# Batch 1's queries loaded four tokens a partition in a retention and GELU-MLP kernel on one Trainium2 core

## The chip, the core and the metric

The kernel runs on one core of a Trainium2 chip. The metric is the device time of one execution in microseconds (us). Before the change the median of 11 runs is 298.6 us, the lowest 297.46 and the highest 299.8. Engines are called as in the profile: PE (matmuls), PEld (its weight loads), DVE (vector), ACT (scalar), POOL (GpSimd), SP (the queue that issues the DMAs).

## What is computed

Eight batches of eight heads, 576 tokens, head dimension 64. First a retention attention: scores with a decay mask, times the values. Its result, tokens by 512, goes through an MLP with 2048 hidden columns and a tanh GELU.

```python
scores = scale * np.matmul(q, k.transpose(0, 1, 3, 2))
gamma = 1.0 - 2.0 ** (-5.0 - np.arange(H, dtype=np.float32))
Dmat = np.where(rel >= 0, gamma[:, None, None] ** rel[None, :, :], 0.0)
ret = scores * Dmat[None, :, :, :]
attn = np.matmul(ret, v)
x = attn.transpose(0, 2, 1, 3).reshape(B * S, H * D)
h = x @ w_in
g = 0.5 * h * (1.0 + np.tanh(c * (h + 0.044715 * h * h * h)))
out = g @ w_out
```

Inputs and output are float32; on the chip the operands of the matmuls are float16.

## The kernel before, in words

**Tiling.** The first 512 tokens of a batch are split in two halves `s` of 256, each in two chunks `c` of 128; the last 64 tokens of each batch are a "tail" that is handled apart. The eight heads are two groups `hh` of four, and a group is two head pairs `pp`. Per half and group, `load_qkv` (L192) fetches 256 KB of q, k or v into a float32 tile; `cast_qk` (L249) or `cast_v` (L258) makes float16 of it and gives the float32 tile back; `tr` (L356) transposes four 128-column blocks on PE and copies them out of PSUM to the tile `T`; `score_mm` (L428) makes the scores of one half and group; `mask_sc` (L446, DVE) multiplies the mask in; `values` (L543) multiplies with v. The part of the past goes through a running state: `state_mm` (L490), `scan` (L513, DVE), `put` (L533, a cast of the state to the block-diagonal tile `tbd`), `inter_mm` (L573). `evac` (L592, DVE) moves the result of a chunk out of PSUM to the tile `x`. Then a block of the MLP: `up` (L633) or `up_half` (L720) with the GELU on ACT, sums and differences of the hidden columns (`mix_sa`, `mix_sc`, `mix_d`, L740 to L754), and seven products with combinations of w_out (`product`, L763, `down`, L866), whose results `settle` (L794) adds up.

**Two layouts of a load.** Normally a partition receives two consecutive tokens of each of four heads (`r=2`), a run of 512 bytes per head. For the pairs in the set `R4` (L128) it receives four consecutive tokens of each of two heads (`r=4`), a run of 1024 bytes; the index `s` of such a load and of its cast and transpose then stands for the head pair, not for the half of the tokens. One such tile feeds both halves, so both tiles of a group, `s` 0 and 1, are needed before the first scores of that group. Its transposes are copied out in two copies of 128x256 instead of one of 128x512. When k is loaded so, `back` (L414) transposes it back for `state_mm`; q needs nothing of the kind.

**What sets the order.** Nothing is scheduled at run time. A list `units` (L1024 to L1027) gives the main work of PE: units 0 to 9 are empty (L1024), 10 and 11 are `up_half` of block 0, 14 to 25 its `up(4)` to `up(15)`, 26 to 41 block 1's `up_half`, 42 to 48 and 49 to 55 the `down` products of blocks 0 and 1, 56 to 71 `up` of block 2, 72 to 78 its products. A dictionary `plan` (L1028 to L1372) hangs further steps behind each unit, each with its engine: A is ACT, V is DVE, G is POOL, S2 is half on ACT and half on DVE. Within a unit the list's order counts. Each engine executes its own queue strictly in this order. Later blocks have a plan of the same kind in a loop (L1378 to L1533).

**Loads.** All loads go through SP's one queue in the order of the calls L903 to L985. A load needs either one of 12 tiles `ld` (L163), which a cast gives back, or a home borrowed from a tile not yet in use (`E`, `E2`, `O`, `H`, L897 to L901 and L1022).

**Padding.** `pads` (L988 to L1014) puts dummy matmuls of 128 columns (`pad`, L145, their line is L150) in front of named steps of batch 0, and `warm(16)` puts some at the start.

Of the kernel before, what the change touches and what calls it, by code (L numbers as in the profile page):

```python
# [19 lines left out]
def kernel(  # L20
# [24 lines left out]
    B, H, S, D = q.shape  # L45
# [52 lines left out]
    sc = const.tile([128, 2 * H + 4], F32, name="sc")  # L98
# [29 lines left out]
    R4 = {(0, "k"), (0, "q")}  # L128
# [762 lines left out]
    def add(plan, *entries):  # L891
# [9 lines left out]
    H = []  # L901
# [15 lines left out]
    load_w_in(0, 2, E)  # L917
# [3 lines left out]
    load_w_in(2, 1, None)  # L921
    load_w_in(1, 0, E2)
# [4 lines left out]
    load_qkv(1, 0, 0, "q", None)  # L927
    load_w_in(2, 3, None)
# [3 lines left out]
    load_qkv(1, 0, 1, "q", None)  # L932
    load_w_in(3, 3, None)
    load_w_in(3, 1, None)
    load_w_in(3, 2, None)
    load_qkv(1, 0, 1, "v", None)
    load_qkv(1, 1, 0, "k", O)
    load_qkv(1, 1, 0, "q", O)
    load_qkv(1, 1, 1, "k", O)
    load_w_out(0, None)  # L940
    load_qkv(1, 1, 0, "v", O)
    load_qkv(1, 1, 1, "q", O)
    load_qkv(1, 1, 1, "v", O)
    load_w_out(1, None)
    load_w_out(6, E3)
    load_w_out(2, None)
# [3 lines left out]
    load_w_out(14, H)  # L950
    load_w_out(7, E3)
    load_w_out(8, O)
    load_w_out(10, H)
    load_w_out(11, H)
    load_w_out(12, H)
    load_w_out(9, O)
    load_w_out(15, H)
# [3 lines left out]
    load_qkv(2, 0, 0, "q", None)  # L961
    load_qkv(2, 0, 0, "k", None)
    load_qkv(2, 1, 0, "q", None)
    load_qkv(2, 0, 1, "q", None)
    load_qkv(2, 0, 0, "v", None)
# [23 lines left out]
        ("tr", 0, 1, 0, 0): 7,  # L989
        ("tr", 0, 1, 1, 0): 0,  # L990
        ("tr", 0, 1, 1, 1): 1,
        ("st", 0, 1, 0): 1,
# [4 lines left out]
        ("bk", 0, 1, 1): 0,  # L997
        ("us", 0, 0): 4,
        ("us", 0, 1): 4,
        ("xs", 0, 0): 7,  # L1000
        ("xs", 0, 1): 0,
        ("in", 0, 3): 0,
        ("tr", 0, 0, 0, 0): 9,
        ("tr", 0, 0, 0, 1): 10,
        ("tr", 0, 0, 1, 0): 23,
        ("tr", 0, 0, 1, 1): 5,
# [3 lines left out]
        ("tr", 0, 1, 0, 1): 5,  # L1010
        ("in", 0, 1): 11,
        ("us1", 0, 1): 0,
        ("in", 0, 2): 7,
# [6 lines left out]
    def turn():  # L1020
# [7 lines left out]
    plan = add({},  # L1028
        (0, L(cast_qk, 0, 0, 0, "q", A)),
        (0, L(new_x, 0)),  # L1030
# [9 lines left out]
        (3, L(score_mm, 0, 1, 0)),  # L1040
        (2, L(back, 0, 0, 0, V)),
# [4 lines left out]
        (2, L(back, 0, 1, 0, A)),  # L1046
        (1, L(tr, 0, 0, 1, 0, S2)),
        (1, L(cast_qk, 0, 1, 1, "q", G)),
        (5, L(back, 0, 0, 1, A)),
        (3, L(tr, 0, 0, 1, 1, A)),  # L1050
        (1, L(cast_qk, 0, 1, 1, "k", G)),
# [4 lines left out]
        (4, L(score_mm, 0, 0, 1)),  # L1056
        (4, L(cast_v, 0, 0, 0, G)),
        (5, L(scan, 0, 0)),
        (5, L(values, 0, 0)),
        (6, L(score_mm, 0, 1, 1)),  # L1060
        (6, L(put, 0, 0, A)),
        (3, L(cast_v, 0, 0, 1, G)),
        (5, L(scan, 0, 1)),
        (1, L(inter_mm, 0, 0, 0)),
        (5, L(put, 0, 1, A)),
# [6 lines left out]
        (6, L(cast_v, 0, 1, 1, G)),  # L1072
        (7, L(state_mm, 0, [1])),
        (5, L(cast_v, 0, 1, 0, G)),
        (7, L(scan, 0, 2)),
# [7 lines left out]
        (11, L(scan, 0, 3)),  # L1083
        (9, L(evac, 0, 1, 1)),
        (7, L(cast_w_in, 0, 3, A)),
        (9, L(F0.up_half, 0, 0)),
        (8, L(cast_w_in, 0, 1, G)),
        (8, L(cast_w_in, 0, 0, G)),
        (11, L(put, 0, 3, V)),
        (9, L(F0.up_half, 1, 0)),  # L1090
        (12, L(cast_qk, 1, 0, 0, "k", G)),
        (14, L(cast_w_in, 2, 3, G)),
        (12, L(cast_qk, 1, 0, 1, "k", V)),
        (7, L(cast_w_in, 1, 3, A)),
        (10, L(cast_w_in, 2, 1, A)),
        (8, L(cast_w_in, 1, 1, A)),
        (13, L(F0.mix_sc, 0, 2, V)),
# [3 lines left out]
        (9, L(cast_w_in, 2, 0, V)),  # L1101
        (18, L(F0.mix_d, 0, 2, V)),
        (7, L(turn)),
        (7, L(cast_w_in, 1, 2, A)),
        (19, L(F0.mix_sc, 2, 2, V)),
        (10, L(cast_qk, 1, 0, 0, "q", A)),
        (18, L(cast_qk, 1, 0, 1, "q", V)),
        (19, L(cast_w_in, 3, 0, A)),
        (19, L(tr, 1, 0, 1, 1, A)),
        (15, L(tr, 1, 0, 1, 0, S2)),  # L1110
        (15, L(tr, 1, 0, 0, 0, S2)),
        (17, L(cast_w_in, 3, 2, G)),
# [4 lines left out]
        (28, L(inter_mm, 1, 0, 0)),  # L1117
# [7 lines left out]
        (22, L(state_mm, 1, [0])),  # L1125
        (21, L(score_mm, 1, 0, 1)),
        (24, L(cast_qk, 1, 1, 0, "k", G)),
# [4 lines left out]
        (21, L(cast_qk, 1, 1, 0, "q", A)),  # L1132
        (22, L(values, 1, 0)),
        (29, L(put, 1, 1, A)),
        (23, L(cast_qk, 1, 1, 1, "q", A)),
        (25, L(cast_v, 1, 1, 0, V)),
        (27, L(F0.mix_sc, 4, 2, G)),
        (25, L(tr, 1, 1, 0, 0, V)),
# [3 lines left out]
        (22, L(F0.mix_sa, 4, 2, G)),  # L1142
        (27, L(cast_v, 1, 1, 1, V)),
        (24, L(tr, 1, 1, 0, 1, A)),
        (28, L(state_mm, 1, [1])),
        (28, L(F0.mix_d, 4, 2, V)),
        (27, L(tr, 1, 1, 1, 0, A)),
# [3 lines left out]
        (27, L(tr, 1, 1, 1, 1, A)),  # L1151
# [4 lines left out]
        (29, L(mix_w_out, 0, "sums", G)),  # L1156
# [3 lines left out]
        (31, L(inter_mm, 1, 1, 0)),  # L1160
        (32, L(mix_w_out, 1, "sums", G)),
        (28, L(mix_w_out, 1, "copy", A)),
        (34, L(mix_w_out, 1, "add", G)),
        (33, L(mix_w_out, 2, "sums", G)),
        (32, L(evac, 1, 1, 0)),
        (32, L(mix_w_out, 3, "sub", V)),
        (37, L(mix_w_out, 3, "copy", A)),
        (33, L(evac, 1, 1, 1)),
        (33, L(mix_w_out, 2, "add", V)),
        (37, L(mix_w_out, 3, "sums", V)),  # L1170
        (33, L(mix_w_out, 1, "sub", V)),
        (40, L(mix_w_out, 7, "add", V)),
        (37, L(mix_w_out, 0, "copy", A)),
        (36, L(mix_w_out, 0, "add", V)),
        (40, L(mix_w_out, 4, "sums", V)),
        (34, L(mix_w_out, 2, "copy", A)),
        (34, L(mix_w_out, 2, "sub", V)),
        (37, L(mix_w_out, 6, "sums", V)),
        (35, L(mix_w_out, 4, "sub", V)),
        (38, L(mix_w_out, 5, "sub", V)),  # L1180
        (43, L(mix_w_out, 4, "add", V)),
        (38, L(mix_w_out, 5, "add", V)),
        (38, L(mix_w_out, 4, "copy", V)),
# [3 lines left out]
        (40, L(mix_w_out, 6, "add", V)),  # L1187
        (36, L(mix_w_out, 7, "sub", V)),
        (33, L(mix_w_out, 6, "copy", A)),
        (42, L(cast_qk, 2, 0, 0, "q", A)),  # L1190
        (29, L(mix_w_out, 7, "copy", A)),
# [3 lines left out]
        (35, L(scan, 1, 3)),  # L1195
        (44, L(cast_v, 2, 1, 0, G)),
        (43, L(cast_qk, 2, 0, 1, "k", A)),
        (42, L(cast_qk, 2, 0, 0, "k", A)),
        (43, L(tr, 2, 0, 0, 1, S2)),
        (40, L(F0.mix_sc, 6, 2, V)),  # L1200
        (41, L(cast_qk, 2, 0, 1, "q", A)),
# [4 lines left out]
        (43, L(F1.mix_sa, 0, 4, V)),  # L1206
        (43, L(tr, 2, 0, 0, 0, A)),
        (44, L(tr, 2, 0, 1, 0, V)),
        (38, L(tiles, 3)),
        (43, L(cast_qk, 2, 1, 0, "k", A)),  # L1210
        (41, L(cast_qk, 2, 1, 0, "q", A)),
        (46, L(cast_tail, 0, "k", G)),
        (44, L(score_mm, 2, 0, 0)),
        (46, L(cast_tail, 0, "q", G)),
        (45, L(F1.mix_sa, 4, 4, V)),
        (45, L(score_mm, 2, 0, 1)),
        (45, L(state_mm, 2, [0])),
        (44, L(mask_sc, 2, 0, 0)),
        (45, L(cast_qk, 2, 1, 1, "q", A)),
        (42, L(tr, 2, 0, 1, 1, V)),  # L1220
        (49, L(scan, 2, 1)),
# [3 lines left out]
        (47, L(cast_tail, 0, "v", G)),  # L1225
        (49, L(put, 2, 0, A)),
        (49, L(cast_qk, 3, 0, 0, "k", A)),
        (47, L(score_tail_mm, 0)),
        (45, L(cast_v, 2, 1, 1, G)),
        (48, L(cast_qk, 3, 0, 0, "q", G)),  # L1230
        (49, L(tr, 2, 1, 1, 1, A)),
        (46, L(tr_tail, 0, A)),
        (47, L(cast_qk, 2, 1, 1, "k", A)),
        (47, L(mask_tail, 0)),
        (48, L(tr, 2, 1, 1, 0, A)),
        (47, L(cast_v, 3, 0, 1, G)),
        (47, L(tr, 2, 1, 0, 1, S2)),
        (48, L(values, 2, 0)),
        (46, L(cast_qk, 3, 0, 1, "q", G)),
        (46, L(cast_v, 3, 0, 0, G)),  # L1240
        (49, L(F0.store)),
        (48, L(cast_tail, 1, "q", G)),
        (48, L(values_tail, 0)),
        (46, L(F1.mix_sc, 0, 2, V)),
        (47, L(tr, 2, 1, 0, 0, A)),
        (48, L(inter_tail, 0)),
        (47, L(F1.mix_sc, 6, 2, V)),
        (48, L(cast_tail, 1, "v", G)),
        (51, L(cast_tail, 1, "k", A)),
        (52, L(cast_qk, 3, 1, 1, "k", G)),  # L1250
# [313 lines left out]
```

## Time and profile before

| | us |
|---|---|
| median of 11 runs | 298.6 |
| lowest, highest run | 297.46, 299.8 |
| the profiled execution, its own time | 298.64 |
| its span, first to last instruction | 296.8 |
| busy in it: PE, PEld | 290.1, 206.9 |
| busy in it: DVE, ACT, POOL | 237.3, 165.8, 96.7 |
| first matmul of the MLP starts | 22.16 |
| last matmul ends, about | 293.4 |

The profile's times count from the first instruction of the span; 1.84 us of the execution lie outside it. A busy PE in it includes the dummy matmuls, which have the lines L139 and L150, and matmuls overlap one another, so that a duration of one is longer than its share: 16 products of 256 columns take 1.75 us from start to start. A line such as L247 is that of a helper (all casts and copies); the tile's name tells what it is.

### The profile page before, as it was taken

The numbers are of one execution on the slowest core, as the hardware profiler recorded it, in microseconds if no ns is written. First come the engines' busy times: TensorE is split into PE (matmuls) and PEld (weight loads), VectorE is DVE, ScalarE is ACT, GpSimd is POOL, SyncE is SP. The second block draws the span as 40 slices with busy tenths as digits, with TensorE's granted clock in tenths as the row PEclk, the third lists the DMA queues.
The fourth block names the chain that finished last, engine by engine and source line by source line (L and its number), as shares of the span: only waits on it lengthen the run. The fifth ranks groups of instructions, "written<-read, shape, count | busy, mean of one in ns | idle before, by whom it ended". The sixth has DMA issues, their size and how long they took to land.

```text
span 296.8 us, 8809 instructions
## 1 busy us (share of the span) xinstructions
PE 290.1 (98%) x3689; PEld 206.9 (70%) x3689; DVE 237.3 (80%) x455; ACT 165.8 (56%) x323; POOL 96.7 (33%) x129
## 2 busy tenths in 40 slices
PE   8989999999999999999999999999999999999995
PEld 5657478888885468655875587558755886787684
DVE  4978879989997989888569846999688198886774
ACT  7559889973746762565445554564445316605830
POOL 4672793055250236056026304799000000000000
PEclk9999999999999999999999999999999999999999
DMA  6999999766789989994998699573120002002204
GB/s 211 334 358 316 316 385 301 199 178 172 206 244 202 280 267 165 261 296 94 208 291 260 86 234 307 157 147 16 43 100 2 1 26 118 2 0 73 71 0 144
DMA packets 92663, 52.48 MB, mean 177 GB/s; under 512 B 38352, under 2 KB 86480, under 8 KB 92624
## 3 DMA queue, kind: packets, MB, share of 16 engines
q1 hardware_dynamic: 92288, 51.26, 64.2%
q10 hardware_dynamic: 336, 0.66, 0.8%
q8 instruction: 29, 0.48, 0.7%
q14 instruction: 10, 0.08, 0.1%
HBM read 36.70 MB, written 9.44 MB: 155 GB/s over the span
## 4 chain that ended last, share of the span: by engine, by line
PE 79%; ACT 6%; DMA 4%; DVE 3%; POOL 3%; issue 2%; SPq 2%; DVEq 0%; POOLq 0%; ACTq 0%
PE hp L641 26%; PE my L783 10%; PE mz L783 9%; PE mu L783 5%; PE mv L783 5%; PE hp L727 5%; PE mw L783 5%; PE py L671 2%; ACT tbd L247 2%; DMA ld<-in_moe_w_in_dram 2%; PE xs L553 2%; PE xs L580 2%; DMA ld<-in_v_dram 2%; PE st L438 2%; POOL cv L260 2%
## 5 line engine op out<-in xcount | busy, mean ns | idle before, releaser
L641 PE MATMUL hp<-x,w_in_sb 128*128 128x512 f16 x400 | 92.6, 379 | 0.5 <-DVE vs L522 0.2
L645 ACT ACTIVATE gT<-hp 128x512 f16<-128x512 f32 x108 | 63.7, 597 | 44.1 <-PE hp L641 43.3
L641 PEld LDWEIGHTS <-w_in_sb 128*128 128x128 f16 x432 | 40.9, 98 | 43.2 <-issue 1.0
L783 PEld LDWEIGHTS <-gT 128*128 128x128 f16 x576 | 55.8, 98 | 8.1 <-ACT gT L714 0.2
L451 DVE TENSOR_TENSOR ret<-st,cm 128x512 f16<-128x512 f32 x64 | 40.1, 683 | 4.3 <-PE st L438 4.0
L260 POOL TENSOR_TENSOR cv<-ld,sc 128x512 f16<-128x512 f32 x28 | 29.9, 1083 | 39.3 <-DMA ld<-in_v_dram 26.0
L247 POOL CAST kq<-ld 128x512 f16<-128x512 f32 x27 | 18.5, 689 | 57.9 <-DMA ld<-in_k_dram 44.8
L247 ACT CAST tbd<-ws 64x256 f16<-64x256 f32 x59 | 23.7, 402 | 21.0 <-DVE ws L526 18.0
L783 PE MATMUL my<-w_out_sb,gT 128*128 128x256 f16 x288 | 34.5, 273 | 0.0
L783 PE MATMUL mz<-w_out_sb,gT 128*128 128x256 f16 x288 | 34.4, 273 | 0.0
L783 PEld LDWEIGHTS <-gsum 128*128 128x128 f16 x288 | 27.9, 98 | 3.4
L752 DVE TENSOR_TENSOR gsum<-gT 128x1024 f16<-128x1024 f16 x35 | 29.0, 829 | 0.4 <-ACT gT L645 0.4
L756 DVE TENSOR_TENSOR gT<-gT 128x1024 f16<-128x1024 f16 x35 | 28.2, 824 | 0.2
L593 DVE TENSOR_TENSOR x<-xs,gx 128x512 f16<-128x512 f32 x32 | 21.7, 684 | 4.6 <-PE xs L580 4.3
L744 DVE TENSOR_TENSOR gdia<-gT 128x512 f16<-128x512 f16 (+1 forms) x32 | 16.6, 520 | 5.7 <-ACT gT L714 2.5
L810 DVE TENSOR_TENSOR ost<-ost,mv 128x512 f32<-128x512 f32 x18 | 11.6, 684 | 11.6 <-issue 7.5
L247 ACT CAST kq<-ld 128x512 f16<-128x512 f32 x27 | 16.4, 616 | 4.8 <-DMA ld<-in_q_dram 3.3
L727 PE MATMUL hp<-x,w_in_sb 128*128 128x256 f16 x160 | 18.8, 273 | 0.0
L783 PE MATMUL mv<-w_out_sb,gsum 128*128 128x256 f16 x144 | 17.2, 273 | 0.0
L783 PE MATMUL mw<-w_out_sb,gdia 128*128 128x256 f16 x144 | 17.2, 273 | 0.0
L783 PE MATMUL mu<-w_out_sb,gsum 128*128 128x256 f16 x144 | 17.2, 273 | 0.0
L727 PEld LDWEIGHTS <-w_in_sb 128*128 128x128 f16 x160 | 15.3, 98 | 2.1 <-issue 0.2
(118 smaller groups left out, 394.9 us busy)
## 6 DMA issues: line engine op xcount, KB each, us to landing
ld<-in_k_dram SPq DMA_DIRECT2D x30, 256.0 KB, 5.2
ld<-in_q_dram SPq DMA_DIRECT2D x30, 256.0 KB, 5.3
ld<-in_v_dram SPq DMA_DIRECT2D x30, 256.0 KB, 5.9
out_dram<-ost SPq DMA_DIRECT2D x14, 512.0 KB, 5.1
loan<-in_moe_w_out_dram SPq DMA_DIRECT2D x12, 256.0 KB, 6.2
loan<-in_moe_w_in_dram SPq DMA_DIRECT2D x8, 256.0 KB, 6.4
ld<-in_moe_w_in_dram SPq DMA_DIRECT2D x8, 256.0 KB, 6.1
ld<-in_moe_w_out_dram SPq DMA_DIRECT2D x4, 256.0 KB, 5.6
```

The source lines that it names most:

```text
L247: (eng.copy if eng is nc.scalar else eng.tensor_copy)(out=out, in_=in_)
L260: eng.tensor_tensor(out=unperm(att[b]["v"][:, s, hh, :]), in0=perm(t), in1=sc[:, 8 * hh : 8 * hh + 8] .rearrange("p (r h) -> p r h", r=2) ...
L451: nc.vector.tensor_tensor(out=x.rearrange("p (a m) -> p a m", a=2), in0=st[hl].rearrange("p (a m) -> p a m", a=2), in1=cm.rearrange("p r s ...
L593: nc.vector.tensor_tensor(out=xb[b][:, :, 2 * s + c].rearrange("p s q i -> p q s i"), in0=att[b]["x", s][c].rearrange("p (q s i) -> p q s ...
L641: nc.tensor.matmul(hp, w_in_sb[:, ct, 128 * f : 128 * f + 128], x[:, :, ct, :], start=(ct == 0), stop=(ct == 3),)
L645: nc.scalar.activation(out=self.g(f // 2)[:, f % 2], in_=hp, func=AF.Gelu_apprx_tanh)
L727: nc.tensor.matmul(hp[:, 256 * h : 256 * h + 256], w_in_sb[:, ct, 256 * j + 128 * h : 256 * j + 128 * h + 128], xb[self.b][:, :, 2 * u : 2 ...
L744: e.tensor_tensor(out=self.sa[:, j : j + n], in0=g[:, :, 0, 0:256], in1=g[:, :, 1, 256:512], op=ALU.add)
L752: e.tensor_tensor(out=self.sc[:, j : j + n], in0=g[:, :, 0], in1=g[:, :, 1], op=ALU.add)
L756: e.tensor_tensor(out=g.rearrange("p j h c -> p j (h c)")[:, :, 256:768].rearrange("p j (h c) -> p j h c", h=2), in0=g[:, :, :, 0:256], in ...
L783: nc.tensor.matmul(t[u] if isinstance(t, list) else t[:, 256 * u : 256 * u + 256], lhs(j, slice(128 * u, 128 * u + 128)), w_out_sb[:, j, w ...
L810: nc.vector.tensor_tensor(out=out, in0=in0, in1=t, op=op)
```

## The change

`(1, "q")` is added to `R4`, so the four q loads of batch 1 get four tokens a partition by head pair. The rest follows or goes with it:

- The loads, casts and transposes of q of both pairs are moved ahead: `cast_qk(1,1,0,"q")` from unit 21 to 12, `cast_qk(1,1,1,"q")` from 23 to 17, `tr(1,1,0,1)` from 24 to 15, `tr(1,1,1,1)` from 27 to 19, and `tr(1,0,1,1)` from 19 to 20.
- The order of the loads of w_in, of batch 1 and of w_out changes.
- The padding changes, from 132 dummy matmuls to 119, and the order of several steps of batch 0.
- Some steps change engine: `put(0,1)` and `put(2,0)` from A to S2, `cast_qk(1,0,0,"q")` and `cast_qk(2,1,1,"k")` from A to G, `cast_qk(3,1,1,"k")` from G to A, `put(2,2)` from A to G, `F2.mix_sa(0)` and `F2.mix_sc(2)` from V to G, `tr_tail(3)` from A to V, `cast_v(4,0,0)` from G to V.
- Some steps move by a few units in blocks 0 to 2 and in the loop.

```diff
-    R4 = {(0, "k"), (0, "q")}
+    R4 = {(0, "k"), (0, "q"), (1, "q")}
...
-    load_w_in(0, 2, E)
     load_w_in(0, 1, E)
     load_w_in(1, 1, E2)
     load_w_in(1, 3, E2)
     load_w_in(2, 1, None)
+    load_w_in(0, 2, E)
...
     load_qkv(1, 0, 0, "q", None)
+    load_qkv(1, 1, 0, "q", O)
     load_w_in(2, 3, None)
     load_qkv(1, 0, 1, "k", None)
     load_w_in(3, 0, None)
     load_qkv(1, 0, 0, "v", None)
     load_qkv(1, 0, 1, "q", None)
+    load_qkv(1, 1, 1, "q", O)
     load_w_in(3, 3, None)
-    load_w_in(3, 1, None)
     load_w_in(3, 2, None)
     load_qkv(1, 0, 1, "v", None)
+    load_w_in(3, 1, None)
     load_qkv(1, 1, 0, "k", O)
-    load_qkv(1, 1, 0, "q", O)
     load_qkv(1, 1, 1, "k", O)
...
-        ("tr", 0, 1, 0, 0): 7,
-        ("tr", 0, 1, 1, 0): 0,
+        ("tr", 0, 1, 0, 0): 3,
+        ("tr", 0, 1, 1, 0): 4,
...
-        ("us", 0, 0): 4,
-        ("us", 0, 1): 4,
+        ("us", 0, 0): 2,
+        ("us", 0, 1): 0,
...
-        (2, L(back, 0, 1, 0, A)),
-        (1, L(tr, 0, 0, 1, 0, S2)),
+        (4, L(back, 0, 1, 0, A)),
+        (0, L(tr, 0, 0, 1, 0, S2)),
...
-        (4, L(cast_v, 0, 0, 0, G)),
+        (2, L(cast_v, 0, 0, 0, G)),
...
-        (6, L(put, 0, 0, A)),
+        (7, L(put, 0, 0, A)),
...
-        (5, L(put, 0, 1, A)),
+        (5, L(put, 0, 1, S2)),
...
-        (10, L(cast_qk, 1, 0, 0, "q", A)),
-        (18, L(cast_qk, 1, 0, 1, "q", V)),
+        (10, L(cast_qk, 1, 0, 0, "q", G)),
+        (16, L(cast_qk, 1, 0, 1, "q", V)),
         (19, L(cast_w_in, 3, 0, A)),
-        (19, L(tr, 1, 0, 1, 1, A)),
+        (20, L(tr, 1, 0, 1, 1, A)),
...
+        (15, L(tr, 1, 1, 0, 1, A)),
+        (17, L(cast_qk, 1, 1, 1, "q", A)),
+        (12, L(cast_qk, 1, 1, 0, "q", A)),
+        (19, L(tr, 1, 1, 1, 1, A)),
...
-        (21, L(cast_qk, 1, 1, 0, "q", A)),
...
-        (23, L(cast_qk, 1, 1, 1, "q", A)),
...
-        (24, L(tr, 1, 1, 0, 1, A)),
...
-        (27, L(tr, 1, 1, 1, 1, A)),
...
-        (49, L(put, 2, 0, A)),
+        (49, L(put, 2, 0, S2)),
...
-        (52, L(put, 2, 2, A)),
+        (52, L(put, 2, 2, G)),
...
-        (64, L(put, 3, 2, A)),
+        (68, L(put, 3, 2, A)),
...
-        (58, L(put, 3, 1, A)),
+        (59, L(put, 3, 1, A)),
```

## Prediction

> **What bounds the kernel now.** I read the page first, then the chain of waits, then the timelines of single engines where the diff touches something.
>
> ```profile
> PE 290.1 (98%) x3689; PEld 206.9 (70%) x3689; DVE 237.3 (80%) x455; ACT 165.8 (56%) x323; POOL 96.7 (33%) x129
> ...
> DMA  6999999766789989994998699573120002002204
> ```
>
> PE looks full, but the start is filled with dummy matmuls. In the PE timeline the first `up_half` starts at 22.16 us; from there PE issues at full rate to about 293.4. So only two things shorten the kernel: an earlier first `up_half`, or fewer stalls of PE after it. The DMA row is at 9 in the first slices, so loads there land in the order of issue, one per fixed time: in the trace's landings a w_in load (2 KB runs) takes 0.67 us, a load with 512-byte runs 0.83 to 0.90, batch 0's four-token q and k (1 KB runs) 0.71 to 0.79.
>
> What holds the first `up_half` is the chain of waits near 20 us, and DVE's timeline behind it:
>
> ```profile
> 18.28 0.40 ACT tbd L247
> ...
> 18.70 0.59 ACT kq L247
> ...
> 19.34 0.38 PE us L506 x16
> ...
> 20.23 0.44 DVE ws L526
> ```
> ```profile
> 20.75 0.29 DVE L247 CAST tbd<-ws 64x256 f16<-64x256 f32 x1
> 21.08 0.43 DVE L247 CAST w_in_sb<-loan 128x512 f16<-128x512 f32 x1
> 21.42 1.49 DVE L593 TENSOR_TENSOR x<-xs,gx 128x512 f16<-128x512 f32 x2
> ```
>
> ACT casts four pieces of state (17.03 to 18.68), only then copies the transposed-back k (`back(0,1,1)`) that `state_mm` needs; then `scan`, `put`, a w_in cast, and `evac(0,0,1)` (21.42 to 22.10), after which `up_half` starts.
>
> The second place is batch 1's scores, where ACT runs in step with PE:
>
> ```profile
> 31.70 0.60 ACT L645 ACTIVATE gT<-hp 128x512 f16<-128x512 f32 x1 [0.27 <-PE hp L641]
> 32.19 0.61 ACT L247 CAST w_in_sb<-ld 128x512 f16<-128x512 f32 x1
> 32.70 0.59 ACT L247 COPY T<-tr 128x512 f16<-128x512 f16 x1
> ```
> ```profile
> 31.50 0.39 PE L361 MATMUL tr<-ident,kq 128*128 128x128 f16 x4
> ...
> 33.99 0.42 PE L438 MATMUL st<-T 64*64 64x128 f16 x16
> ...
> 37.55 0.40 PE L580 MATMUL xs<-T,tbd 128*128 128x128 f16 x4 [0.15 <-ACT tbd L247]
> ```
>
> The copy ends at 33.29, 0.7 us before the scores at 33.99 read it: no stall. `inter_mm` at 37.55 does wait, 0.32 us, for `put(1,0)`. The third place is the end of block 1:
>
> ```profile
> 86.77 0.39 PE L580 MATMUL xs<-T,tbd 128*128 128x128 f16 x4
> ...
> 89.47 0.45 PE L566 MATMUL xs<-rett,cvt 64*64 64x64 f16 x8 [0.27 <-DVE rett L479]
> ```
>
> PE stalls there some 0.6 us in all for DVE, which has no gap over 0.1 us from 65.6 to 93.7.
>
> **What the Trainium skill says.** "Perfetto Trace Analysis", Identifying the Most-Contended Engine: matmul busy share does not tell how near the limit a kernel is. Agrees: 98% here with 22 us of mostly padding. "TensorE: Matmul & The Clock Gate", Back-to-back issue gap: N/2.4 + 2.5 ns, 109 ns for N = 256. The trace has 16 products in 1.75 us, 109 each; so PE after 22 us can only gain by stalls. "DMA: Bandwidth & Descriptors", Why small descriptors are slow: a fixed overhead per packet. The 0.85, 0.74 and 0.67 us above agree in direction. "SBUF — State Buffer", Who interferes with whom: a DVE operation with two SBUF inputs blocks a GpSimd read until it ends. Fits POOL's 128x512 casts, 0.61 us at best, 1.07 at worst; used for the third rival.
>
> **The change, part by part.**
>
> *Loads.* Four q loads at 0.74 for 0.85 us: 0.45 us of DMA time saved. It shows only where a load is waited for on PE's path, so I price it at nothing. Their issues on SP cost as much as before (about 0.46 us each, two moved past six to ten others) and SP is five to six us ahead of the landings. w_in(0,2) falls from place 15 to 19, landing about 19.4 instead of 16.7; cast on POOL by 20.1, needed after 21: hidden by 1 us. w_in(3,1) falls from place 32 to 36. Adding the durations above from w_in(2,0), which landed at 22.97, it lands near 31.9 (before 29.3); its cast comes in ACT's queue at about 32.6: hidden by 0.7. If it came later, each us would be one of PE. k(1,0,1), cast by DVE, lands 0.75 later, at 26.0, in front of the mixes; the 0.78 us gap that DVE has at 27.13 and two units of slack cover it.
>
> *Start of batch 0.* (a) 11 fewer dummies stand before the first scores, but these need `tr(0,1,0,1)`, now behind `tr(0,0,1,0)`, whose k is cast at 8.56: first scores about 10.2 as now, gain 0. (b) `back(0,1,0)` moves behind ACT's five copies, `cast_v(0,0,0)` goes first and starts at 11.4 instead of 13.04: `back(0,0,1)` is copied by 14.3 instead of 14.97, fewer dummies precede `state_mm`, and it ends near 14.7, not 15.5. DVE's masks end at 15.0, so `scan` starts 0.55 earlier. (c) `put(0,1)` half on DVE takes one 0.41 cast out of ACT's four; with (b) `back(0,1,1)` is copied by 18.3 instead of 19.29, a gain of 1.0. DVE pays 0.29, but its mask ends at 18.6, before `scan` at 18.7. (d) DVE's w_in(1,0) cast may not start before that load lands, 20.10: it now starts at 20.15, not 21.08. `evac` ends 21.2, first `up_half` near 21.25: **-0.90**. Bounds 0 and -1.3.
>
> *ACT queue at the second scores.* ACT receives the q(1,1) casts early (0.51 of pitch each; one q(1,0) cast leaves to POOL), and `tr(1,1,0,1)`, `tr(1,1,1,1)`. Four-token copies are two of 128x256 (0.26 apart, 0.37 to 0.41 each, from batch 0). With E the end of `up(9)`: GELU at E+0.20, w_in(3,0) cast +0.69, copies of `tr(1,1,1,1)` +1.20 and +1.46, w_in(3,1) cast +1.77, GELU +2.28, copies of `tr(1,0,1,1)` +2.77 and +3.03, ending E+3.44. PE needs them after a transpose, scores, `up`, a transpose, `up`: before 2.49, now 2.75. Queued behind the copies: score, masks, `scan`, `put(1,0)`. **+0.75**; bounds 0 and 1.1. Behind it the chain scores, two masks, `scan`, `put`, `inter_mm` is unchanged; it lands near 37.45 instead of 37.55, but PE has 0.44 us of transposes already behind it: 0.54 gained up to there, so **-0.39** for stalls that were there anyway (0.32, and ACT's two casts gone).
>
> *DVE.* `put(2,0)` half on DVE, 0.29 us inside the stretch where DVE never rests: **+0.29**, bounds 0 and 0.29. Other swaps there are order alone, 0.
>
> *POOL.* `put(2,2)` is now behind three casts. v(3,1,1) starts at 83.72 in the timeline; half a us earlier it is 83.2, then 1.03 + 0.8 + 1.2, so 86.2. No POOL cast of 64x256 is in the trace; the nearest is 128x256 at 0.40, the worst 128x512 at 1.07. Two at 0.40 end at 87.0, PE waits 0.75, and the stall for DVE that follows shrinks by as much: **0**. Nothing speaks for a gain; upper end +1.6 (third rival).
>
> *Later puts.* `put(3,1)` and `put(3,2)` leave the units where four state casts (101.36, 1.65 us) and two (94.58, 0.82 us) precede GELUs; PE stalls 0.36 at 96.5 and 0.30 at 103.2, and `tr_tail(3)` leaves ACT: **-0.50**, bounds 0 and -0.66. The loop's swaps move `evac(b,0,1)` two units later; its PSUM bank isn't asked for before unit 11: 0. `F2` mixes on POOL (2 us each) are used 5 or more units later: 0.
>
> Sum: -0.90 + 0.75 - 0.39 + 0.29 + 0 - 0.50 = **-0.75**. Against the profiled 298.64 us that is 297.9; the median, 298.6, is the same to 0.04.
>
> **Rivals.**
> 1. *ACT keeps up.* Without the 0.75 at the scores: -0.90 - 0.39 - 0.50 + 0.15 = -1.64, 297.0. For it: ACT had 0.27 us gaps before four GELUs. Against: the six entries between are strictly in order.
> 2. *Late gain absent.* The casts of state just delay other GELUs: -0.54 + 0.29 = -0.25, 298.4.
> 3. *POOL's state cast decides (slower).* v(3,1,1) lands no earlier than before and POOL's casts take 1.07 under DVE's traffic: `put(2,2)` ends at 86.7 + 2.14 = 88.8, `inter_mm` waits until then; with 0.40 for it and the tail's scores and 1.75 for the product, the tail's values come at 91.0 instead of 89.4: +1.6, 299.5. It decides from an end of `put(2,2)` after 87.25; from 88.55 the kernel is slower than 299.2. For it: POOL waited 4.45 us for that load. Against: one-input casts of 128x256 took 0.40 everywhere.
> 4. The change does do what it says: all four q loads precede the first scores; no rival there.
>
> **How the numbers follow.** 0.2% is 0.6 us, about what a measurement of this kernel tells from no change. Forecast 0.38 (range 297.3 to 298.5; faster 0.27, same 0.09, slower 0.02); rival 1 0.20 (faster); rival 2 0.11 (0.03, 0.07, 0.01); rival 3 0.31 (slower 0.27, same 0.04). Faster 0.50, same 0.20, slower 0.30. Range 296.6 (rival 1 with 1.3 at the start) to 299.7.
>
> **What would show it.** First `up_half` near 21.25; four-token q landings 0.74 apart; a PE stall of 0.75 ahead of the second scores (about 34.3) with ACT busy without a gap; `inter_mm` near 37.45; `put(2,2)` on POOL with its end against 87.25; no stalls of 0.3 near 96 and 103. Wrong if the start gains nothing, or if w_in(3,1) lands after 33, or if stalls of PE appear in the loop.

## The result and the profile after

The kernel after takes 300.5 us in the median of 12 runs (299.5 to 302.5). Runs of the kernel before on the same chip have a median of 298.39 us (47 runs, 297.46 to 300.29). The ratio is 1.0078 with a 95% interval from 1.0061 to 1.0094: the change makes the kernel slower by 0.8%, and the forecast of 297.9 us and its range are both missed. A second series of 18 runs has a ratio of 1.0048, so after costs 1.4 to 2.3 us. The profiled execution of after is the fastest of its runs (299.5 us, span 297.4); a second one, taken later of the same kernel, has 300.4 us and a span of 298.3.

Not all of the cost can be seen in a profile. The time outside the span, ahead of the first instruction or behind the last, is 2.11 us in the mean of the 12 runs and 2.12 in that of the 18, against 1.80 in 39 runs of before. So about 0.3 us of the loss lies there.

First the two rows of the page that the prediction began with:

```profile
PE 289.9 (97%) x3687; PEld 206.8 (70%) x3687; DVE 240.6 (81%) x457; ACT 163.1 (55%) x320; POOL 102.0 (34%) x133
...
DMA  6999999567889969994996899473120003002204
```

POOL has 5 us more work, DVE 3 us more and ACT 3 us less. PE's share says nothing, as before. What says something is the list of what PE waited for (us in total, times, longest; the entry for the dummy matmuls at the start is left out):

```profile
PE st L438 <- ACT T L247: 0.7, 1, 0.7
...
PE tr L361 <- DVE rett L479: 0.4, 1, 0.4
PE xs L553 <- DVE ret L451: 0.4, 2, 0.2
PE mv L783 <- DVE gsum L752: 0.2, 1, 0.2
```

Such a list leaves out the short waits. To see where time is lost for good, I counted the columns of all matmuls of the MLP in order of time and read off when the same count is reached in two traces. Each row says by how much after is later than before at a place (negative is earlier). A stall that is absorbed later shows as a step up and a step down, one that stays as a step up alone:

| at the place of before | after, profile of 299.5 us | after, profile of 300.4 us |
|---|---|---|
| first `up_half`, 22.2 us | -0.71 | -0.18 |
| 28 us (transposes of q moved ahead) | -0.48 | +0.04 |
| 34 us (second scores of batch 1) | +0.48 | +1.00 |
| 42 us | -0.33 | +0.29 |
| 50 us (values of group 1) | -0.02 | +0.61 |
| 75 us | +0.50 | +0.80 |
| 90 us | +0.49 | +0.38 |
| 104 us (late puts) | -0.03 | -0.14 |
| 116 us (product `mv` of block 2) | +0.39 | +1.28 |
| 240 us | +0.35 | +1.25 |
| end | +0.61 | +1.51 |

From 116 to 240 us nothing moves: the edits in the loop cost nothing there. Three things in the table have no experiment of their own. Both traces lose another 0.26 us at 243 us, in front of a small product of the last block (L671), where the profile names no wait; p_both and p_both_sp below, which have none of the loop's edits, lose 0.2 us at the same place. The step at 73 us is 0.51 us in the first profile and 0.19 in the second. And the row at 90 us leans on before's profile: PE's wait at 89.47 us, which the prediction shows, is found again in only two of the 14 other profiles whose units 49 to 56 are those of before. The other 12 come up on before's profile there by 0.38 to 0.53 us; after comes up by 0.14 and 0.25.

The rest is four places, which I take in the order of the prediction.

*Start.* DVE's timeline of after (start, us, engine, line, operation, tiles) answers to the lines of 20.75 to 21.42 before:

```profile
16.02 1.15 DVE L247 CAST tbd<-ws 64x256 f16<-64x256 f32 x1
17.20 0.69 DVE L593 TENSOR_TENSOR x<-xs,gx 128x512 f16<-128x512 f32 x1
17.81 1.28 DVE L451 TENSOR_TENSOR ret<-st,cm 128x512 f16<-128x512 f32 x2
...
20.05 0.29 DVE L247 CAST tbd<-ws 64x256 f16<-64x256 f32 x1
20.37 0.43 DVE L247 CAST w_in_sb<-loan 128x512 f16<-128x512 f32 x1
```
```profile
15.11 1.92 POOL L133 MEMSET tbd<- 128x512 f16 x4
```

Half of `put(0,1)` takes 1.15 us, where the same half of a later put, at 20.05, takes 0.29. Beside it POOL zeroes the second `tbd` tile. Masks and `scan` come later by the difference.

*Second scores.* ACT's timeline of after, and PE's:

```profile
31.71 0.61 ACT L247 CAST w_in_sb<-ld 128x512 f16<-128x512 f32 x1
32.22 0.65 ACT L247 COPY T<-tr 128x256 f16<-128x256 f16 x2
32.74 0.64 ACT L247 CAST w_in_sb<-ld 128x512 f16<-128x512 f32 x1
33.26 0.62 ACT L645 ACTIVATE gT<-hp 128x512 f16<-128x512 f32 x1
33.75 0.67 ACT L247 COPY T<-tr 128x256 f16<-128x256 f16 x2
```
```profile
32.55 0.39 PE L361 MATMUL tr<-ident,kq 128*128 128x128 f16 x4
...
34.47 0.42 PE L438 MATMUL st<-T 64*64 64x128 f16 x16 [0.67 <-ACT T L247]
...
37.67 0.40 PE L580 MATMUL xs<-T,tbd 128*128 128x128 f16 x4
```

ACT works without a gap, as forecast, and the scores wait for the copies. `inter_mm` starts at 37.67, no longer behind a wait of its own.

*Block 1's end.* `put(2,2)` on POOL takes 0.85 us for both halves and ends at 86.44, before the 87.25 from which the third rival decided:

```profile
85.59 0.85 POOL L247 CAST tbd<-ws 64x256 f16<-64x256 f32 x2 [1.63 <-DVE ws L526]
```

*Product `mv` of block 2.* The second profile of after shows the largest single step of the table. DVE, then POOL, then PE:

```profile
108.43 1.74 DVE L744 TENSOR_TENSOR gdia<-gT 128x512 f16<-128x512 f16 x1
110.09 1.52 DVE L756 TENSOR_TENSOR gT<-gT 128x1024 f16<-128x1024 f16 x1
...
113.88 2.41 DVE L752 TENSOR_TENSOR gsum<-gT 128x1024 f16<-128x1024 f16 x1
```
```profile
107.33 2.56 POOL L752 TENSOR_TENSOR gsum<-gT 128x1024 f16<-128x1024 f16 x1
...
113.62 2.11 POOL L756 TENSOR_TENSOR gT<-gT 128x1024 f16<-128x1024 f16 x1
```
```profile
116.34 1.27 PE L783 MATMUL mv<-w_out_sb,gsum 128*128 128x256 f16 x10 [1.23 <-DVE gsum L752]
```

While POOL does the `mix_sc(2)` that it received, DVE's `gdia` takes 1.74 us instead of 0.41, and the two operations after it are stretched as well. So DVE reaches `mix_sc(6)` (the `gsum` at 113.88) 1.4 us later than before, and there it takes 2.41 us itself, beside POOL's difference. The product that reads it waits. In before the same product ran through:

```profile
114.42 1.91 PE L783 MATMUL mv<-w_out_sb,gsum 128*128 128x256 f16 x16
```

### The profile page after: what moved, and what is told of

Same layout as the page of the kernel before. It is cut to its first block, busy times and chain, and to the rows that moved or that the text cites. A ratio compares the mean times of both kernels' runs of the same rounds, so it can differ in the third digit from the quotient of the medians.

```text
span 297.4 us, 8814 instructions
## 1 busy us (share of the span) xinstructions
PE 289.9 (97%) x3687; PEld 206.8 (70%) x3687; DVE 240.6 (81%) x457; ACT 163.1 (55%) x320; POOL 102.0 (34%) x133
## 4 chain that ended last, share of the span: by engine, by line
PE 68%; DVE 13%; DMA 12%; SPq 3%; ACT 2%; issue 1%; DVEq 0%
PE hp L641 25%; PE my L783 8%; PE mz L783 7%; PE mu L783 5%; PE mv L783 5%; PE mw L783 4%; DMA loan<-in_moe_w_out_dram 3%; PE hp L727 3%; PE py L671 2%; DVE ret L451 2%; DMA loan<-in_v_dram 2%; DMA ld<-in_v_dram 2%; DMA ld<-in_moe_w_in_dram 2%; DVE ost L810 2%; DVE gsum L752 2%; DMA ld<-in_q_dram 2%
## 5 line engine op out<-in xcount | busy, mean ns | idle before, releaser
L260 POOL TENSOR_TENSOR cv<-ld,sc 128x512 f16<-128x512 f32 x27 | 30.6, 1145 | 23.4 <-DMA ld<-in_v_dram 23.4
L247 ACT CAST tbd<-ws 64x256 f16<-64x256 f32 x55 | 22.0, 403 | 24.9 <-DVE ws L526 24.2
L756 DVE TENSOR_TENSOR gT<-gT 128x1024 f16<-128x1024 f16 x35 | 30.8, 898 | 0.2
L247 ACT CAST kq<-ld 128x512 f16<-128x512 f32 x26 | 15.7, 616 | 1.2 <-DMA ld<-in_k_dram 0.7
```

The costliest lines, as they stand in the source:

```text
L247: (eng.copy if eng is nc.scalar else eng.tensor_copy)(out=out, in_=in_)
L260: eng.tensor_tensor(out=unperm(att[b]["v"][:, s, hh, :]), in0=perm(t), in1=sc[:, 8 * hh : 8 * hh + 8] .rearrange("p (r h) -> p r h", r=2) ...
L756: e.tensor_tensor(out=g.rearrange("p j h c -> p j (h c)")[:, :, 256:768].rearrange("p j (h c) -> p j h c", h=2), in0=g[:, :, :, 0:256], in ...
```

## The experiments

The theory after reading these traces: the queue of ACT and the mixes on POOL cost more than the start and the late puts bring. Its rivals are that the start itself costs, or that the order of the loads does.

**Where along the program.** Four kernels: after once more, and three that are after up to a unit and before from there on (c10: padding and units 0 to 9; c32: also the four-token q, its loads and units up to 31; c57: all loads, units up to 56).

```diff
 # c10: after's padding and plan for units 0 to 9, all else before
-        ("us", 0, 0): 4,
-        ("us", 0, 1): 4,
+        ("us", 0, 0): 2,
+        ("us", 0, 1): 0,
...
-        (5, L(put, 0, 1, A)),
+        (5, L(put, 0, 1, S2)),
```

> The changed kernel once more, for a second profile and times on the same chip as the three below. Median 300.4 us, 2.0 above before. Both theories expect stalls of PE in a typical execution that the first profile (299.5 us, the fastest of its runs) does not have: theory A (the loads' new order) puts them before 60 us, where casts wait for landings; theory B (work moved to POOL) after 60 us.

> The start alone: padding and the lists of units 0 to 9 as in the changed kernel (one w_in cast of unit 9 left in place), everything else as before. Both theories: first up_half at 21.4 instead of 22.2 and 0.7 us gained to the end, 297.7. A rival says that what is won at the start is lost again by unit 32, since loads or DVE set the pace there: then 298.4 as before.

> Units 0 to 31, padding, four-token q and the loads up to batch 1's last as in the changed kernel; units 32 on, the later loads and the loop as before. Theory A (the loads' new order and the entries of units 10 to 31 cost, more in some executions than in others): 299.5 to 300.5. Theory B (the later moves cost): 298.1, that is the 0.7 of the start less 0.4 at the second scores.

> Units 0 to 56 and all loads as in the changed kernel, units 57 on (block 2 and the loop) as before. Theory A: as c32 within 0.3, 299.5 to 300.5. Theory B: 299.3 if the cost is in block 1 (put(2,0), put(2,2)), 298.1 if it is in block 2 (mixes on POOL).

| kernel | median us | ratio to before | 95% interval |
|---|---|---|---|
| after_again | 300.29 | 1.0048 | 1.0033 to 1.0064 |
| c10 | 298.89 | 1.0008 | 0.9996 to 1.0021 |
| c32 | 299.86 | 1.0051 | 1.0034 to 1.0068 |
| c57 | 300.6 | 1.0071 | 1.0049 to 1.0093 |

Most of the cost is there by unit 31. But the start alone gains nothing, though its profile is ahead of before by 0.36 us at the first `up_half` and by 0.99 at 90 us (0.53 of this is the stall at 89 us that before's own profile has). It loses 1.65 us near 278 us, in the last block, which the change doesn't touch. ACT's timeline of c10 shows where:

```profile
274.91 3.03 ACTq L834 DMA_DIRECT2D out_dram<-ost  x3
277.98 0.59 ACT L689 COPY q<-pv 128x512 f32<-128x512 f32 x1 [2.61 <-PE hp L641]
```

ACT issues four stores of the tails' output; three of them take 3.03 us, and the copy L689 that product `py` waits for is queued behind them. The same group in c10 and in before (count: shortest, median and longest in ns, first and last start); in c57 the longest is 1401 ns:

```profile
L834 ACTq DMA_DIRECT2D out_dram<-ost x4: 382/432/2082, 274.5 to 277.5; - x4
```
```profile
L834 ACTq DMA_DIRECT2D out_dram<-ost x4: 377/434/435, 275.5 to 276.9; - x4
```

I come back to this below.

**The middle and the late part alone.** m32 has the loads, four-token q and units 10 to 31 of after on the start of before. m32m puts ACT's cast of w_in(3,1) behind the copies that the scores need, and its load earlier. lateputs has three edits of the late part. a_f2v is after with the two mixes back on DVE.

```diff
 # m32m against m32
+    load_w_in(3, 1, None)
     load_w_in(3, 2, None)
     load_qkv(1, 0, 1, "v", None)
-    load_w_in(3, 1, None)
...
-        (19, L(cast_w_in, 3, 1, A)),
         (20, L(tr, 1, 0, 1, 1, A)),
+        (20, L(cast_w_in, 3, 1, A)),
 # lateputs against before
-        (58, L(put, 3, 1, A)),
+        (59, L(put, 3, 1, A)),
...
-        (61, L(tr_tail, 3, A)),
+        (61, L(tr_tail, 3, V)),
...
-        (64, L(put, 3, 2, A)),
+        (68, L(put, 3, 2, A)),
 # a_f2v against after
-        (59, L(F2.mix_sa, 0, 2, G)),
+        (59, L(F2.mix_sa, 0, 2, V)),
...
-        (67, L(F2.mix_sc, 2, 2, G)),
+        (67, L(F2.mix_sc, 2, 2, V)),
```

> The kernel before with the four-token q, the load order of the first 41 loads and units 10 to 31 of after; start, padding, later units and loop of before. Theory: the queue of ACT at the second scores of batch 1 costs 0.8 to 1.1 us there, of which 0.3 is given back by stalls that were there anyway: 299.1 to 299.5 us, ratio 1.002 to 1.003. Rival: the cost comes only with the earlier start, which makes these loads and casts late by comparison: 298.4 to 298.8, same as before.

> m32, but the load of w_in(3,1) goes back ahead of that of w_in(3,2), and its cast on ACT comes behind the copies of the transposed q(1,0,1) instead of ahead of them. Theory (the order of ACT's queue, and in some executions the late landing of w_in(3,1), holds the second scores): they start 0.5 to 0.7 us earlier than in m32 and the time is 298.3 to 298.8, 0.4 to 0.8 under m32. Rival: PE then waits as long in the next product for this cast or at the values of group 1 near 46.8 us: the same as m32 within 0.2.

> The kernel before with three edits alone: put(3,1) in unit 59 instead of 58, put(3,2) at the head of unit 68 instead of unit 64, tr_tail(3) on DVE. Theory of the prediction: the stalls of 0.36 and 0.30 us near 96.5 and 103.2 go, 298.0 to 298.3. Rival: the gain is there at 104 us, but DVE, which has 0.4 us more, is later at mix_sc(6) and product mv near 114 waits for it: 298.5 to 298.8.

> The kernel after, with F2's mix_sa(0) and mix_sc(2) back on DVE. Theory: on POOL these two-input operations stretch the DVE operations beside them (gdia 1.74 us instead of 0.43, mix_d 1.53 instead of 0.68 in the second profile of after), so that DVE reaches mix_sc(6) late and product mv waits 0.4 to 1.3 us for it near 114 us. Then that stall is gone here and the time is 299.1 to 299.8 us, 0.5 to 1.2 under after's 300.3 to 300.5. Rival: DVE has 1.1 us more work of its own and is just as late: 300.2 to 300.6.

| kernel | median us | ratio to before | 95% interval |
|---|---|---|---|
| m32 | 299.13 | 1.0028 | 1.0015 to 1.0042 |
| m32m | 299.16 | 1.0025 | 1.0012 to 1.0038 |
| lateputs | 298.11 | 0.9983 | 0.9969 to 0.9996 |
| a_f2v | 299.17 | 1.0021 | 1.0009 to 1.0034 |

m32 costs 0.28% by itself, so it needs no early start. m32m's scores do start earlier: 12.50 us after its first `up_half` instead of 13.03 in m32. The time is the same, as the rival said. PE's timelines show why, m32's first, then m32m's:

```profile
35.08 0.42 PE L438 MATMUL st<-T 64*64 64x128 f16 x16 [0.67 <-ACT T L247]
...
47.17 0.46 PE L553 MATMUL xs<-ret,cv 64*64 64x128 f16 x17
47.82 0.41 PE L553 MATMUL xs<-ret,cv 64*64 64x128 f16 x15 [0.18 <-DVE ret L451]
```
```profile
34.89 0.42 PE L438 MATMUL st<-T 64*64 64x128 f16 x16
...
47.36 0.46 PE L553 MATMUL xs<-ret,cv 64*64 64x128 f16 x17
48.10 0.41 PE L553 MATMUL xs<-ret,cv 64*64 64x128 f16 x15 [0.28 <-DVE ret L451]
```

Counted from its first `up_half`, the values of group 1 start at 25.12 us in m32 and at 24.97 in m32m: of the 0.53 only 0.15 is left, and the wait for the masks inside the values is longer by 0.1. DVE's four masks in a row (45.58 to 48.05 in m32m) bind there. In before the 32 matmuls of the values ran through:

```profile
46.90 0.64 PE L553 MATMUL xs<-ret,cv 64*64 64x128 f16 x32
```

lateputs gains what the prediction said: 0.17% or 0.5 us by the ratio, 0.34 in the medians, and 0.52 in its progress between 90 and 104 us. PE's timelines, before first, then lateputs:

```profile
96.86 1.02 PE L641 MATMUL hp<-x,w_in_sb 128*128 128x512 f16 x4 [0.16 <-DVE vs L522]
...
102.52 1.75 PE L641 MATMUL hp<-x,w_in_sb 128*128 128x512 f16 x6
```
```profile
96.88 1.04 PE L641 MATMUL hp<-x,w_in_sb 128*128 128x512 f16 x4
...
102.55 2.32 PE L641 MATMUL hp<-x,w_in_sb 128*128 128x512 f16 x10
```

The wait at 96.86 is gone, and from 102.55 on ten products take 2.32 us, where six took 1.75.

a_f2v is 1.1 us under after_again in the median and 1.3 under the first series of after (0.27% and 0.57% by the ratios). In its profile `gdia` is short again, and `mv` has all its matmuls in one group without a wait, DVE first:

```profile
109.53 0.41 DVE L744 TENSOR_TENSOR gdia<-gT 128x512 f16<-128x512 f16 x1
...
113.45 0.87 DVE L752 TENSOR_TENSOR gsum<-gT 128x1024 f16<-128x1024 f16 x1
```
```profile
114.80 1.91 PE L783 MATMUL mv<-w_out_sb,gsum 128*128 128x256 f16 x16
```

**The start, the stores of the tail, and the parts still open.** In the kernels from here on, whose names begin with p_, plain copies stand in for the transposing DMAs of later batches. They leave out the transposition of q and k there, so only their times mean something, and p_before is the control. The copies aren't neutral: in all ten profiles of such kernels PE falls back by 0.3 to 0.8 us between 120 and 200 us, where the others stay within 0.04 us. So these kernels are compared with each other. p_startz is c10 with the zeroing moved, p_both adds the three edits of lateputs, p_f2g is lateputs with the two mixes on POOL. In those ending in _sp, SP issues all eight stores of the tail. p_c32l moves one load against p_c32, and p_u49 has units 49 to 56 of after alone.

```diff
 # p_before against before (four such calls, nine DMAs)
-        nc.sync.dma_start_transpose(
+        nc.sync.dma_start(
 # p_startz against c10, beside the copies
-        (7, L(tbd_zero, 1, G)),
+        (12, L(tbd_zero, 1, G)),
 # p_f2g against lateputs, beside the copies
-        (59, L(F2.mix_sa, 0, 2, V)),
+        (59, L(F2.mix_sa, 0, 2, G)),
-        (67, L(F2.mix_sc, 2, 2, V)),
+        (67, L(F2.mix_sc, 2, 2, G)),
 # p_before_sp, p_startz_sp, p_both_sp
-                    (nc.sync if b % 2 else nc.scalar).dma_start(
+                    nc.sync.dma_start(
 # p_c32l against p_c32
+    load_w_in(3, 1, None)
     load_w_in(3, 2, None)
     load_qkv(1, 0, 1, "v", None)
-    load_w_in(3, 1, None)
 # p_u49 against p_before, the two steps that the prediction priced
-        (49, L(put, 2, 0, A)),
+        (49, L(put, 2, 0, S2)),
-        (52, L(put, 2, 2, A)),
+        (52, L(put, 2, 2, G)),
 # and one of the moves there
-        (49, L(F1.mix_d, 6, 2, V)),
+        (50, L(F1.mix_d, 6, 2, V)),
```

> The kernel before with the nine transposing DMAs of q and k of batches 3 to 7 and their tails replaced by plain DMA copies of the same size, so that the scores of these batches are made from q and k that are not transposed. It is the control for three kernels with the same replacement. All theories: the copies land earlier than they are needed, as the transposes did, and the time is that of before, 298.2 to 298.8 us. If it is lower, the transposes were waited for.

> p_before (plain copies instead of the transposing DMAs of batches 3 to 7) with the padding and units 0 to 9 of after, as in c10, and with the zeroing of the second tbd tile on POOL (four memsets of 0.52 us) in unit 12 instead of unit 7. Theory: these memsets stretch the half of put(0,1) on DVE (1.05 to 1.15 us instead of 0.29) and so held back masks and scan; now that half takes 0.3 us, the first up_half lies near 21.3 us, and the time is 0.4 to 0.9 us under p_before's. Rival: the landing of w_in(1,0) (19.7 to 20.3) or POOL's later casts hold it, or an earlier start gives nothing in the time: within 0.2 us of p_before or over it, as c10 was.

> p_startz and the three edits of lateputs (298.11 us, ratio 0.9983) together, with the same plain copies. Theory: both gains add up, 0.9 to 1.4 us under p_before. Rival: only the late puts count, 0.4 to 0.6 under p_before.

> The kernel lateputs with F2's mix_sa(0) and mix_sc(2) on POOL instead of DVE, as in after, and with the same plain copies. Theory: the operations of DVE beside them are stretched, mix_sc(6) comes late and product mv near 114 us waits for it: 0.1 to 0.9 us over p_before. Rival: without the rest of the change (cast_v(4,0,0) on DVE and the order of DVE's steps) DVE has room for it: 0.3 to 0.6 under p_before, as lateputs.

> p_before (plain copies for the transposing DMAs) with all eight stores of the tail block issued by SP, none by ACT. It is the control of p_startz_sp. In p_before's profile the four issues on ACT take 0.38 to 0.44 us each and PE doesn't wait: within 0.3 us of p_before's 298.7, if such executions are typical. If it is 0.5 us or more lower, the issues on ACT cost the kernel before too.

> p_startz (299.3 us) with all eight stores of the tail block issued by SP. Theory (what the early start gains is given back where ACT issues these stores, in front of the copy that product py waits for): 0.6 to 1.5 us under p_startz, and 0.3 us or more under p_before_sp. Rival (the start's gain isn't there in most executions): no change by over 0.3 us, and no gain over p_before_sp.

> c32 (start and units 10 to 31 of after, 299.86 us, ratio 1.0051) with the plain copies. Control of p_c32l: 299.8 to 300.4 us.

> p_c32 with one edit: the load of w_in(3,1) goes ahead of that of w_in(3,2), where it lies two loads earlier (some 1.6 us earlier landing). Theory: in typical executions of the early start this load lands after 33 us, and ACT, which casts it ahead of the copies that the second scores need, waits for it: 0.4 to 1.0 us under p_c32. Rival: the landing is in time in most executions (32.3 us in after's profile): within 0.2 us of p_c32.

> p_before (298.7 us) with units 49 to 56 of after alone: put(2,0) half on DVE, put(2,2) on POOL and the order of the steps there. The prediction: +0.29 us, 298.8 to 299.1. Rival (put(2,2) on POOL ends after 87.25 in most executions, as at 87.74 in a_f2v's profile): 299.2 to 299.8. Second rival: PE's wait for DVE near 89 us swallows all of it, 298.4 to 298.7.

> p_both (start with the zeroing later, and the three late edits; 299.06 us) with the eight stores of the tail block issued by SP. Theory: start and late puts add up once the issues on ACT are gone: 297.3 to 297.8, 0.3 to 0.7 under p_startz_sp (298.05). Rival: the late puts give nothing beside the earlier start: 297.9 to 298.2.

| kernel | median us | ratio to before | 95% interval |
|---|---|---|---|
| p_before | 298.68 | 1.0013 | 1.0000 to 1.0027 |
| p_startz | 299.31 | 1.0024 | 1.0005 to 1.0043 |
| p_both | 299.06 | 1.0019 | 1.0003 to 1.0034 |
| p_f2g | 299.16 | 1.0030 | 1.0016 to 1.0044 |
| p_before_sp | 298.42 | 0.9997 | 0.9986 to 1.0009 |
| p_startz_sp | 298.05 | 0.9985 | 0.9971 to 1.0000 |
| p_c32 | 300.59 | 1.0068 | 1.0046 to 1.0090 |
| p_c32l | 300.65 | 1.0075 | 1.0051 to 1.0099 |
| p_u49 | 299.66 | 1.0030 | 1.0011 to 1.0049 |
| p_both_sp | 297.62 | 0.9969 | 0.9953 to 0.9985 |

*The zeroing.* With the memsets out of the way the half of `put(0,1)` takes 0.29 us and the first `up_half` of this profile of p_startz starts at 20.49 us, DVE first, then PE:

```profile
15.90 0.29 DVE L247 CAST tbd<-ws 64x256 f16<-64x256 f32 x1
```
```profile
20.49 0.71 PE L727 MATMUL hp<-x,w_in_sb 128*128 128x256 f16 x5
```

The mechanism is shown, and over all profiles the mean of the first `up_half` is 22.38 us with the start of before (8 profiles, 21.88 to 22.91), 21.87 with that of after (8, 21.45 to 22.06) and 21.20 with the zeroing moved (4, 20.49 to 21.70). The memsets, now at 21.3 us, stretch another operation there: DVE's cast of w_in at 21.72 takes 1.74 us instead of 0.43. The time doesn't follow: instead of the 0.4 to 0.9 us expected under its control, p_startz is 0.6 us over it in the medians, 0.11% by the ratios, with intervals that overlap. p_both, expected 0.9 to 1.4 us under, is no faster than p_before either.

*The stores.* The same kernel with the stores on SP is 1.26 us faster than p_startz (0.39% by the ratios), while for the kernel before the same edit is worth 0.26 (0.16%). With the stores on SP the start is worth 0.37 us over its control (298.05 against 298.42), which the intervals leave open, and start and late puts together 0.80 (297.62), where they do not overlap. So in p_startz a gain was given back at ACT's issues. That the start's own gain then reaches the end is not shown: p_both_sp's profile is 1.01 us ahead at the first `up_half` and loses 1.28 at 36 us, where the values wait for DVE's masks. Of ten profiles with the padding of after and stores on ACT, six show one issue of 1.06 to 2.08 us; of seven with the padding of before, none does. In each of the six a transfer of the instruction queue, one of about 16 KB, begins between 0.23 us ahead of the slow issue and 0.23 us into it. In the others it begins 1.5 us or more ahead of the first of them, but for c32's profile, where it begins 0.1 us before the last issue ends and none is slow. The Trainium skill, "Runtime: NRT & Kernel Launch", Instruction fetch mechanics, says that instructions are fetched in blocks of 16 KiB and that crossing into the next is mostly hidden. In these six profiles such a block lands among DMA issues, and an issue takes 0.6 to 1.6 us longer. That the fetch causes the delay is not isolated; that the issues on ACT cost the time is.

*Load order.* p_c32 and p_c32l are alike, so the late landing of w_in(3,1), which one profile (c57) shows at 33.93 us, is not what their time is made of. Both profiles have the slow issue instead, of 1.75 and 1.33 us. PE's waits in p_c32:

```profile
PE py L671 <- DVE q L690: 1.3, 1, 1.3
```

That may be why c32 costs more than m32 in the time (0.23% by the ratios); c32's own profile, of the fastest of its runs, doesn't have it.

*Mixes on POOL.* p_f2g is 0.5 us over p_before, where lateputs was 0.3 to 0.5 under before: 0.8 to 1.0 us for two steps. In its profile PE's lead over before falls from 1.02 to 0.47 us near 106, in lateputs' it doesn't move there (0.26 and 0.24). The place is another one than in after: here DVE's cast of k beside POOL's `mix_sc` took 1.73 us, where it took 0.68 in lateputs, and the score of the tail waited for the `evac` behind it.

*Units 49 to 56.* p_u49 is 1.0 us over p_before in the medians; by the ratios it is 0.17%, 0.5 us, and the intervals overlap. Its `put(2,2)` on POOL ends at 86.77, so the third rival doesn't decide here either (in a_f2v's profile it ended at 87.74 and PE waited 0.4 us for it). The stall lies earlier. PE, then DVE:

```profile
82.22 0.22 PE L506 MATMUL us<-cv,kq 64*64 64x64 f16 x2
82.73 0.44 PE L506 MATMUL us<-cv,kq 64*64 64x64 f16 x30 [0.30 <-DVE ret L451]
```
```profile
79.60 0.68 DVE L593 TENSOR_TENSOR x<-xs,gx 128x512 f16<-128x512 f32 x1
80.20 1.28 DVE L756 TENSOR_TENSOR gT<-gT 128x1024 f16<-128x1024 f16 x2
81.40 1.87 DVE L451 TENSOR_TENSOR ret<-st,cm 128x512 f16<-128x512 f32 x3
```

Two differences `mix_d` stand between the `evac` and the first mask, where p_before has one, and the masks begin 1.5 us earlier there:

```profile
79.93 2.47 DVE L451 TENSOR_TENSOR ret<-st,cm 128x512 f16<-128x512 f32 x4
```

Step L506 waits for one of them.

## Why the prediction was wrong, step by step

The forecast was a sum of -0.75 us; measured part by part it is about +2 (start c10 +0.2, middle m32 +0.8, units 49 to 56 +0.5, late puts -0.5, mixes +1.0), and after itself +1.4 to +2.3 in two series. These parts come from different series and each is uncertain by 0.4 to 0.8 us. That they add up is in part luck: c10's +0.2 contains a loss at ACT's issues that neither profile of after has, and some 0.3 us of after's loss lies outside the span, where c10, m32, p_u49 and lateputs show nothing (1.79 to 1.83 us, as before).

1. **"F2 mixes on POOL (2 us each) are used 5 or more units later: 0."** This is the step that failed most: +1.0 us. I asked only when the results are used and not what the operations do to DVE meanwhile. The Trainium skill's "SBUF — State Buffer", Who interferes with whom, was in my text, but only for POOL's casts in the third rival. It holds in the other direction too: whichever engine holds the ports they share makes the other wait. The trace of before had the price. DVE's mixes, the first while POOL rests, then POOL's:

```profile
108.59 0.68 DVE L752 TENSOR_TENSOR gsum<-gT 128x1024 f16<-128x1024 f16 x1
...
112.45 1.57 DVE L752 TENSOR_TENSOR gsum<-gT 128x1024 f16<-128x1024 f16 x1
114.06 2.50 DVE L756 TENSOR_TENSOR gT<-gT 128x1024 f16<-128x1024 f16 x1
```
```profile
113.43 2.57 POOL L756 TENSOR_TENSOR gT<-gT 128x1024 f16<-128x1024 f16 x1
```

A sum or a difference of this size takes DVE 0.68 us where POOL rests. A mix on POOL relieves DVE of 0.68 or 0.41 us and stretches what runs beside it by 1.3 (`gdia`, 1.74 for 0.41), and more if a second one falls in.

2. **Start, "-0.90".** Part (c) had the half of `put(0,1)` at 0.29 us. It took 1.15 in after's profile, because of the memsets beside it, and the first `up_half` came 0.5 us earlier on average instead of 0.9. Moving the zeroing shows that the rest of the step was right: 1.2 us earlier in the mean of four profiles. What I couldn't see is that in other kernels the gain goes to ACT's issues at 275 us. In the two profiles of after it does not, so there some of the start's gain stays.

3. **Second scores, "+0.75", and "-0.39 for stalls that were there anyway".** The mechanism and the size are right: the scores wait 0.67 us in after's timeline; in m32's progress the wait costs 0.74 us and the two transposes moved ahead 0.22 each, and of these 1.18 us 0.81 is back by 42 us, which leaves 0.37 where the forecast had 0.36. What failed is that the account ended at `inter_mm`. The transposes that left the stretch near 42 us had also covered DVE's masks there, and the values of group 1 then wait: +0.42 near 47 us. So the middle costs 0.8 us. That w_in(3,1) would cost if it landed after 33 us is seen in c57's profile (33.93, cast at 33.95, scores 35.65), but it isn't what the time is made of.

4. **"DVE put(2,0) half +0.29", "other swaps there are order alone, 0".** Mis-sized: with its neighbours it cost about 0.5 by the ratios, though not clear of noise. The swaps put a difference in front of a mask that PE waits for; in a stretch where DVE never rests, order is time.

5. **`put(2,2)` on POOL, "0", and the third rival.** On POOL right in after: 0.85 us for both halves, done at 86.44. But the 0 also took it that "the stall for DVE that follows shrinks by as much", and this stall, read from one profile, is missing in 12 of the 14 others. And the put ends late in some executions: in a_f2v's profile, one of five with this code, PE waits 0.4 us for it. The time of 299.5 that the third rival gave was near the result by luck: its mechanism wasn't the cause in after's profiles.

6. **Later puts, "-0.50".** Right: lateputs is 0.17% faster, 0.5 us, and both profiles of after gain between 90 and 104 us (0.52 in each). The second rival falls.

7. **Loop, 0, and loads, 0.** Right. Between 120 and 240 us the progress of after against before stays within 0.04 us, and the four q loads land 0.72 to 0.73 us behind the load before them.

The chance of 0.30 for slower was nearly all on the third rival (0.27). No case had the work on POOL slowing DVE.

**What stays open.** No experiment isolates the 0.3 us outside the span. It is there in c57 (2.10 us), in part in p_f2g (2.01) and a_f2v (1.94), and not in the other kernels (1.78 to 1.83). The gap of PE at 243 us and the cause of the slow issue on ACT are open as well.

**What beats both.** lateputs, before with three edits, has 0.9983 (0.9969 to 0.9996). The largest gain is p_both_sp with 0.9969 (0.9953 to 0.9985), which adds the early start with the zeroing moved and the stores on SP. It has the plain copies, whose control is 1.0013, so a version with the transposes may do no worse; that one wasn't run, and it is not shown.

## What to carry to other kernels

When a step moves to POOL, ask what DVE has beside it: two of DVE's operations can each lose more than the moved one was worth, and the trace of the kernel before shows the stretched pairs if you look for the same operation with two durations. When a wait is costed, follow PE until the next place where it used to arrive last; work moved out of a stretch uncovers the engine that it hid. And when a gain is in the profile but not in the time, compare progress over the whole span and several executions, of the kernel before too: a gain may be given back in code that nobody touched, and a stall of the one profile you read may be missing in most executions.

## What the runs showed of the hardware

- A cast of 64x256 on DVE (0.29 us) took 1.15 us in after, 1.05 in its second profile, beside memsets on POOL, and 0.29 once these were moved. Beside the moved memsets a cast of 128x512 took 1.74 instead of 0.43 (p_startz).
- DVE operations with both inputs in SBUF took 1.52 to 2.50 us beside a mix on POOL, against 0.41 and 0.68 alone. A cast of 128x512 on DVE took 1.73 beside it (p_f2g), against 0.41 to 0.43 alone.
- One DMA issue on ACT took 1.06 to 2.08 us instead of 0.43 where a 16 KB transfer of the instruction queue started within a quarter of a us of it, in six profiles. In c10, which differs from before in the padding and the first ten units alone, this transfer at the other end of the kernel comes 0.65 us behind the first of the issues, in before 2.2 us ahead of it; in after it comes 1.5 us ahead.
- The time outside the span was 1.78 to 1.83 us in the mean of the runs of most kernels, and 2.11 in after; what sets it is open.
- The first `up_half` of kernels with the same start varies between profiles by 0.6 to 1.2 us. The landings of the first loads vary too: the third landed between 5.00 and 6.93 us. That the one follows from the other is not shown.
